# Transposing k and q by DMA instead of on TensorE in a sliding-window attention and gated feed-forward kernel

## The chip, the cores and the metric

The kernel runs on one core of one Trainium2 chip. The time is the device time of one execution in microseconds (us). The kernel before takes 276.5 us (median of its first three runs, 276.16 to 277.33). Smaller is better. On one core a single run has no second core to be compared with, so a run counts as undisturbed ("fast") unless it is over 1.5% above the fastest of its kernel. All ratios below use fast runs; a median quoted is that of all runs (e1, e8, e12 and e13 have one slow run each).

## The reference, cut to what matters

```python
B, H, S, D = 4, 8, 768, 64           # batch, heads, sequence, head width
scores = q @ k.T / sqrt(D)           # kept where key < 4 (the sink) or 0 <= query - key < 128 (the window)
a = softmax(scores)                  # a row at a time
x = (a @ v)                          # heads side by side: 3072 tokens x 512
out = (relu(x @ w_gate) * (x @ w_val)) @ w_out     # 512 -> 1536 -> 512
```

Inputs and outputs are float32. The kernel computes in bfloat16 with float32 accumulation.

## The kernel before

The attention is cut into units of one head pair each. Units 0 to 7 are the first batch in two halves, kinds "L" and "M". Units 8 to 19 are the twelve head pairs of the other three batches, kind "F", and only these change. For each unit the queue of the sync engine (SP) loads float32 k, q and v. GpSimd casts them to bf16. TensorE transposes k and q, so that the head width lies on the partitions, and ScalarE copies the result out of PSUM:

```python
def load_kq(self, eng):                       # partition p holds n consecutive tokens: pieces of n*64*4 B
    ...
        eng.dma_start(out=dst[0:pp, :, :],
                      in_=x[b, 2*p:2*p+2, r0:r0+pp*nn, :].rearrange("h (p n) d -> p h (n d)", n=nn))

def T(self, pool, shape, tag, qcopy=nc.scalar.copy):
    both = pool.tile(shape, BF16, name="tkq", tag=tag)
    for t in range(kn_): nc.tensor.transpose(ps[:, ...], self.kn_[0:kp, t, :, :]..., ident[0:kp, 0:kp])
    for t in range(qn_): nc.tensor.transpose(pq[:, ...], self.qn_[0:qp, t, :, :]..., ident[0:qp, 0:qp])
    nc.scalar.copy(kT[s]..., ps...)
    qcopy(qT[s]..., pq...)
    ...                                       # VectorE copies the keys that share a tile with the sink: kTs
```

The attention of a unit is a list of stages. Stages are placed between the chunks of the feed-forward (96 chunks; a chunk is four gate and four value matmuls) by a plan. `PLAN` holds pairs (chunk, number of stages issued by then):

```python
def t():
    if nxt is not None: nxt.T(*AT)            # transpose the next unit
    if x >= 5: held(x + 8 - 5)                # a memset on VectorE, then the load of unit x+3
    if at(x + 3) is not None: casts(at(x + 3), "kqv")
    if NP < x < NP + 4: load_wo(x - NP - 1)   # a third of the output weights, cast by the DMA, from GpSimd
...
return [s(0), v, s(1), t, s(2), lambda: norm(u, 0)]      # kind "F"; v ends the unit before
PLAN = ((0, 0), (2, 0), (10, 19), (23, 43), (47, 67), (71, 89), (72, 90))
```

`kT`, `qT` and `kTs` have two buffers each. Scores, outputs and transposes share two PSUM buffers ("at").

The softmax here doesn't subtract the row's maximum and nothing guards it: scores larger than these inputs give would overflow.

Of the kernel before, what the change touches and what calls it, by code (L numbers as in the profile page):

```python
# [43 lines left out]
def kernel(  # L44
# [12 lines left out]
    nc = tc.nc  # L57
    B, H, S, D = q.shape
# [23 lines left out]
    kT = [const.tile([128, 872], BF16, name=f"kT{i}") for i in range(2)]  # L82
    kTs = [const.tile([128, 3, 128], BF16, name=f"kTs{i}") for i in range(2)]
    qT = [const.tile([128, S], BF16, name=f"qT{i}") for i in range(2)]
# [11 lines left out]
    def bc(ap, n):  # L96

        return bass.AP(ap.tensor, ap.offset, [ap.ap[0], [0, n], *ap.ap[1:]])

    class Unit:  # L100
# [26 lines left out]
        def load_kq(self, eng):  # L127

            b, p = self.b, self.p
            for x, dst, r0, pp, nn in ((k, self.staging("k"), self.kr, self.kp, self.kn),  # L130
                                       (q, self.staging("q"), self.qr, self.qp, self.qn)):
                eng.dma_start(out=dst[0:pp, :, :],
                              in_=x[b, 2 * p:2 * p + 2, r0:r0 + pp * nn, :].rearrange("h (p n) d -> p h (n d)", n=nn))

# [29 lines left out]
        def sinkv(self, eng):  # L164

            t = self.sink
            src = vsink[:, self.p, :, :] if self.kind == "M" else self.vn[0:4, 0, :, 0:64]
            eng.tensor_copy(self.vn[0:4, t[0]:t[-1] + 1:2, :, 0:64], bc(src, len(t)))

        def T(self, pool, shape, tag, qcopy=nc.scalar.copy):  # L170

# [88 lines left out]
    def load_wo(c):  # L260
        nc.gpsimd.dma_start(out=wo[:, 4 * c:4 * c + 4, :],
                            in_=moe_w_out.rearrange("(ko ki) n -> ki ko n", ki=128)[:, 4 * c:4 * c + 4, :])
# [37 lines left out]
    def norm(u, part, pool=ps_at):  # L300

        c0, w = u.parts[part][0:2]
        nb = w // 32
        lo, hi = (max(c0, u.q0), min(c0 + w, u.q0 + u.n))
        o, sums = u.V(part, pool)
        r = rpool.tile([128, 2, 416], F32, name="R")
        rc = dpool.tile([128, 13], F32, name="rc")
        nc.vector.transpose(r[:, 0, 0:w], sums[:, 0:w])  # L308
        nc.vector.reciprocal(rc[:, 0:nb], r[:, 0, 0:w].rearrange("p (b j) -> p b j", j=32)[:, :, 0])  # L309
        a = rc[:, 0:nb]  # L310
        nc.vector.transpose(r[:, 1, 0:w], bass.AP(a.tensor, a.offset, [a.ap[0], [1, nb], [0, 32]]))  # L311
        ready[u.b, u.p] = hi
        nc.vector.tensor_tensor(xTs[u.b][:, u.p, lo:hi], o[:, lo - c0:hi - c0], r[:, 1, lo - c0:hi - c0], op=Alu.mult)  # L313
# [36 lines left out]
    with tc.manual_schedule():  # L350
# [3 lines left out]
        AT = (ps_at, [128, 2, 1024], "at")  # L354

        def at(x):
            return U[x] if 0 <= x < len(U) else None

        def casts(u, what):
            for w in what:  # L360
                u.cast(w, nc.gpsimd)
# [15 lines left out]
        def held(x):  # L377

            if x < len(U):
                nc.vector.memset(U[x].stg[0:1, 0:1], 0.0)  # L380
                load(x)
# [62 lines left out]
        def unit_stages(x):  # L444
            u, prev, nxt = U[x], at(x - 1), at(x + 1)

            def s(gi):
                def f():
                    if gi == 0 and u.kind == "F" and u.p == 0:
                        xTs[u.b] = xpool.tile([128, NP, S], BF16, name="xT")  # L450
                    u.S(gi)
                return f

            def v():
                if x > NP:
                    norm(prev, len(prev.parts) - 1)

            def t():
                if nxt is not None:
                    nxt.T(*AT)  # L460
                if x >= 5:
                    held(x + 8 - 5)
                if at(x + 3) is not None:
                    casts(at(x + 3), "kqv")
                if NP < x < NP + 4:
                    load_wo(x - NP - 1)
            if u.kind == "M":
                return [s(0), v, t, s(1)]
            return [s(0), v, s(1), t, s(2), lambda: norm(u, 0)]
# [9 lines left out]
        HALF = {0: ((0, 376), (376, 392))}  # L479
        ORDER = [(0, h, m) for h, m in [(h, m) for h in range(2) for m in range(FM)]]  # L480
        ORDER += [(b, h, m) for b in range(1, B) for h in range(2) for m in range(FM)]
        PLAN = ((0, 0), (2, 0), (10, 19), (23, 43), (47, 67), (71, 89), (72, 90))

        def want(ci):
            for (c0, w0), (c1, w1) in zip(PLAN, PLAN[1:]):
                if ci <= c1:
                    return w0 + (w1 - w0) * (ci - c0) // (c1 - c0)
            return total
# [56 lines left out]
```

## Time and profile before

| Engine | busy us of 273.9 | share |
|---|---|---|
| TensorE (PE) | 259.8 | 95% |
| VectorE (DVE) | 148.2 | 54% |
| ScalarE (ACT) | 129.6 | 47% |
| GpSimd (POOL) | 67.8 | 25% |

These are the busy times of one profiled execution. A TensorE at 95% only says where to look: matmuls overlap, so what an instruction really takes of TensorE is read from the start of one group to the start of the next. The DMA engines are the other thing to watch. They are nearly always busy until 68 us, and after 94 us they are mostly idle.

### The profile page before, as it was taken

The page shows a single profiled execution, that of the slowest core. Times are in us where ns is not written, and L with a number is a line of the kernel's source. Part 1 is how long each engine was busy: PE and PEld are TensorE (multiplying, and loading weights), DVE is VectorE, ACT ScalarE, POOL GpSimd, SP SyncE. Part 2 cuts the span into 40 slices and gives each one's busy share as a digit, 9 for nine tenths or more (in the row PEclk, how much of TensorE's full clock was granted, in tenths as well). Part 3 has the DMA queues.
Part 4 walks back from the last instruction along what each step waited for, and adds up shares of the span by engine and source line. Part 5 has one row for each costly group of instructions (what it writes and reads, how often), then busy time and mean ns, then how long its engine had stood idle before and what let it go on. Part 6 is the DMA issues. An engine that isn't in the chain of part 4 may idle for free.

```text
span 273.9 us, 5552 instructions
## 1 busy us (share of the span) xinstructions
PE 259.8 (95%) x2158; PEld 148.4 (54%) x2158; DVE 148.2 (54%) x329; ACT 129.6 (47%) x218; POOL 67.8 (25%) x123
## 2 busy tenths in 40 slices
PE   5997899899989999999999999999999999999994
PEld 4564555555545555555565555555655555555541
DVE  2486355778797755465666646565474722222210
ACT  3743656666646544536435363644535333323321
POOL 7973547653441330030402105000000000000000
PEclk9999999999999999999999999999999999999999
DMA  8999999998465170531707125101101110011122
GB/s 196 260 224 207 246 255 231 254 251 189 114 172 162 54 212 10 159 84 44 209 4 212 41 75 142 38 0 41 38 2 38 41 38 10 28 42 38 38 77 78
DMA packets 46858, 31.20 MB, mean 114 GB/s; under 512 B 28400, under 2 KB 43760, under 8 KB 46832
## 3 DMA queue, kind: packets, MB, share of 16 engines
q1 hardware_dynamic: 40224, 25.93, 34.2%
q0 software_dynamic: 5808, 4.72, 11.0%
q8 instruction: 17, 0.28, 0.4%
q10 hardware_dynamic: 800, 0.20, 0.3%
q14 instruction: 9, 0.07, 0.1%
HBM read 29.26 MB, written 6.29 MB: 130 GB/s over the span
## 4 chain that ended last, share of the span: by engine, by line
PE 84%; DVE 8%; ACT 3%; issue 1%; DMA 1%; POOL 1%; SPq 0%; DVEq 0%; ACTq 0%
PE gp L323 22%; PE op L342 22%; PE vp L329 21%; PE ops L248 7%; PE sps L226 5%; PE sps L221 2%; DVE R L311 2%; PE tkq L180 2%; DVE R L308 2%; PE tkq L183 2%; DVE xT L313 2%; ACT ee L230 2%; DMA stg<-in_q_dram 1%; DVE ee L232 1%; DVE rc L309 1%
## 5 line engine op out<-in xcount | busy, mean ns | idle before, releaser
L326 ACT ACTIVATE gs<-gp 128x384 f32<-128x384 f32 (+2 forms) x96 | 47.3, 493 | 73.2 <-PE gp L323 71.4
L323 PE MATMUL gp<-xT,wg 128*128 128x384 bf16 (+2 forms) x384 | 78.8, 327 | 1.4 <-DVE xT L313 1.4
L331 DVE TENSOR_TENSOR hT<-gs,vp 128x384 bf16<-128x384 f32 (+2 forms) x96 | 52.7, 549 | 49.3 <-PE vp L329 42.1
L329 PE MATMUL vp<-xT,wv 128*128 128x384 bf16 (+2 forms) x384 | 78.1, 326 | 0.0
L342 PE MATMUL op<-wo,hT 128*128 128x512 bf16 x288 | 75.9, 379 | 0.0
L230 ACT ACTIVATE ee<-sps 128x1006 bf16<-128x1006 f32 (+4 forms) x52 | 46.3, 905 | 26.5 <-PE sps L226 26.5
L329 PEld LDWEIGHTS <-wv 128*128 128x128 bf16 x384 | 37.6, 98 | 26.4 <-issue 1.6
L323 PEld LDWEIGHTS <-wg 128*128 128x128 bf16 x384 | 32.5, 98 | 25.2 <-issue 4.3
L342 PEld LDWEIGHTS <-hT 128*128 128x128 bf16 x288 | 28.2, 98 | 25.1
L232 DVE TENSOR_TENSOR ee<-ee,msk 128x1006 bf16<-128x1006 bf16 (+2 forms) x36 | 26.0, 723 | 26.0 <-ACT ee L230 25.8
L153 POOL CAST kn<-stg 128x768 bf16<-128x768 f32 (+2 forms) x20 | 15.4, 768 | 72.9 <-DMA stg<-in_k_dram 48.7
L346 ACT COPY ot<-op 128x512 f32<-128x512 f32 x24 | 14.1, 586 | 21.6 <-PE op L342 21.5
L308 DVE STREAM_TRANSPOSE R<-ops 128x384 f32<-128x384 f32 (+1 forms) x28 | 16.4, 584 | 14.3 <-PE ops L248 14.3
L186 ACT COPY kT<-tkq 128x768 bf16<-128x768 bf16 (+2 forms) x20 | 14.0, 700 | 18.1 <-PE tkq L183 17.9
L157 POOL CAST vn<-stg 128x768 bf16<-128x768 f32 (+2 forms) x20 | 14.4, 720 | 22.7 <-DMA stg<-in_v_dram 16.7
L311 DVE STREAM_TRANSPOSE R<-rc 128x384 f32<-128x384 f32 (+1 forms) x32 | 18.6, 582 | 1.1
L248 PEld LDWEIGHTS <-ones 128*64 128x64 bf16 x280 | 12.1, 109 | 12.3 <-issue 7.4
L313 DVE TENSOR_TENSOR xT<-ops,R 128x384 bf16<-128x384 f32 (+2 forms) x32 | 17.8, 557 | 1.4
L226 PEld LDWEIGHTS <-kT 64*128 64x128 bf16 x136 | 6.6, 93 | 19.2 <-issue 16.8
L248 PE MATMUL ops<-ee,ones 128*64 128x251 bf16 (+9 forms) x256 | 14.3, 238 | 2.2 <-DVE xT L313 1.3
L226 PE MATMUL sps<-qT,kT 64*128 64x251 bf16 (+3 forms) x136 | 15.5, 250 | 0.8 <-ACT qT L188 0.8
L153 POOL CAST qn<-stg 128x768 bf16<-128x768 f32 (+2 forms) x20 | 14.5, 724 | 5.2 <-DMA stg<-in_q_dram 4.8
(53 smaller groups left out, 169.8 us busy)
## 6 DMA issues: line engine op xcount, KB each, us to landing
out_dram<-ot SPq DMA_DIRECT2D x24, 256.0 KB
stg<-in_k_dram SPq DMA_DIRECT2D x12, 384.0 KB
stg<-in_q_dram SPq DMA_DIRECT2D x12, 384.0 KB
stg<-in_v_dram SPq DMA_DIRECT2D x24, 192.0 KB
wg<-in_moe_w_gate_dram POOLq DMA_DIRECT2D x4, 384.0 KB, 9.7
wv<-in_moe_w_val_dram POOLq DMA_DIRECT2D x4, 384.0 KB, 11.8
wo<-in_moe_w_out_dram POOLq DMA_DIRECT2D x3, 512.0 KB, 5.9
stg<-in_k_dram SPq DMA_DIRECT2D x4, 280.0 KB
```

Of the source, the lines that this page charges most:

```text
L153: cp(dst[0:pp, 0:nn, :, :], self.staging(what)[0:pp, :, :].rearrange("p h (n d) -> p n h d", d=64))
L226: nc.tensor.matmul(out=ps[:, h, c:c + w], lhsT=self.kw(j, r), rhs=qT[s][r, qa:qa + w], start=not biased, stop=True, skip_group_check=True)
L230: nc.scalar.activation(x, ps[:, :, 0:c], Act.Exp, bias=0.0, scale=scale)
L232: nc.vector.tensor_tensor(x, x, bc(msk[:, m0:m0 + c], 2), op=Alu.mult)
L248: nc.tensor.matmul(out=ps[1 - what][64 * h:64 * h + 64, qa - q0:qa - q0 + w], lhsT=self.vn[:, j, h, :] if what else ones[:], rhs=ee[s][:, ...
L311: nc.vector.transpose(r[:, 1, 0:w], bass.AP(a.tensor, a.offset, [a.ap[0], [1, nb], [0, 32]]))
L313: nc.vector.tensor_tensor(xTs[u.b][:, u.p, lo:hi], o[:, lo - c0:hi - c0], r[:, 1, lo - c0:hi - c0], op=Alu.mult)
L323: nc.tensor.matmul(out=gp[:, 0:n], lhsT=wg[:, ko, m * 128:(m + 1) * 128], rhs=x[:, ko, c0:c0 + n], start=ko == 0, stop=ko == KO - 1)
L326: nc.scalar.activation(gs[:, 0:n], gp[:, 0:n], Act.Relu, bias=0.0, scale=1.0)
L329: nc.tensor.matmul(out=vp[:, 0:n], lhsT=wv[:, ko, m * 128:(m + 1) * 128], rhs=x[:, ko, c0:c0 + n], start=ko == 0, stop=ko == KO - 1)
L331: nc.vector.tensor_tensor(hT[:, m, c0:c0 + n], gs[:, 0:n], vp[:, 0:n], op=Alu.mult)
L342: nc.tensor.matmul(out=op, lhsT=hTs[b][:, m, t * 128:(t + 1) * 128], rhs=wo[:, m, :], start=m == 0, stop=m == FM - 1)
```

## The change

Its intent is to take the 144 transposes off TensorE and the 24 copies off ScalarE. A DMA transposes each unit's k, and another its q, from SBUF to SBUF. So that the result has its columns in the order of tokens, partition p must hold tokens p, 128+p, 256+p and so on, and so the load of k and q now reads pieces of one token (64 floats, 256 B).

```diff
@@ load_kq
+                if self.kind == "F":
+                    eng.dma_start(out=dst.rearrange("p h (t d) -> p (h t) d", d=64),
+                                  in_=x[b, 2 * p:2 * p + 2].rearrange("h (t p) d -> p (h t) d", p=128))
+                    continue
@@ new methods of a unit
+        def X(self):
+            for x, dst in ((self.kn_, kT[self.s]), (self.qn_, qT[self.s])):
+                nc.sync.dma_start_transpose(out=dst[:, 0:S].rearrange("d (t r) -> d t r", r=128),
+                                            in_=x[:].rearrange("r t h d -> r (t h d)"))
+        def sinkk(self):
+            ...                      # the two copies into kTs, on VectorE, as before
@@ stage s(0) of unit u
+                    if gi == 0 and nxt is not None and nxt.kind == "F":
+                        nxt.X()
@@ stage t
-                    nxt.T(*AT)
+                    if nxt.kind == "F":
+                        nxt.sinkk()
+                    else:
+                        nxt.T(*AT)
-        PLAN = ((0, 0), (2, 0), (10, 19), (23, 43), (47, 67), (71, 89), (72, 90))
+        PLAN = ((0, 0), (2, 0), (11, 19), (23, 42), (47, 66), (71, 89), (72, 90))
```

More of the change, by code (lines that the diff above doesn't have):

```diff
@@ L168, in sinkv @@
             eng.tensor_copy(self.vn[0:4, t[0]:t[-1] + 1:2, :, 0:64], bc(src, len(t)))
+        def X(self):
[3 more added lines that the diff above has]
+        def sinkk(self):
+            s, nt = self.s, len(self.sink)
+            c = 124 * self.sink[0] + 4
+            a = kT[s][:, c:c + 124]
+            nc.vector.tensor_copy(kTs[s][:, 0:nt, 4:128],
+                                  bass.AP(a.tensor, a.offset, [a.ap[0], [248, nt], [1, 124]]))
+            nc.vector.tensor_copy(kTs[s][:, 0:nt, 0:4], bc(kT[s][:, 0:4], nt))
         def T(self, pool, shape, tag, qcopy=nc.scalar.copy):
```

## The prediction

> **What bounds the kernel now.** I read the page's first two parts, then the busy time of each engine in four stretches, then TensorE's timeline, and last the timelines of the DMA-issuing queue and of GpSimd. The page first: TensorE is busy 95% of the span, and no other engine is over 54%.
>
> ```profile
> span 273.9 us, 5552 instructions
> PE 259.8 (95%) x2158; PEld 148.4 (54%) x2158; DVE 148.2 (54%) x329; ACT 129.6 (47%) x218; POOL 67.8 (25%) x123
> ...
> PE   5997899899989999999999999999999999999994
> ...
> DMA  8999999998465170531707125101101110011122
> ```
>
> The average hides three regimes. The stretches show them (columns: window in us, length, busy us of each engine with its instruction count, clock, DMA share, GB/s):
>
> ```profile
> 45.00:94.00 49.00, 45.74 (x480) 27.70 (x480) 40.01 (x86) 29.43 (x43) 22.81 (x36) 1.00 0.76 187
> 94.00:193.00 99.00, 99.00 (x812) 55.30 (x810) 56.50 (x121) 47.91 (x79) 16.22 (x25) 1.00 0.30 88
> 193.00:274.00 81.00, 77.06 (x491) 41.61 (x488) 28.31 (x55) 27.64 (x51) 0.00 (x0) 1.00 0.11 40
> ```
>
> From 94 to 193 us TensorE never stops: 99.00 of 99. Whatever is taken off it there comes off the time one for one. From 45 to 94 us it lacks 3.26 us, VectorE is 82% busy (40.01 of 49), and the DMA engines are at 76%. After 193 us there is no transpose and no unit left to load, so nothing of the change reaches that stretch.
>
> **What one unit's transposes cost on TensorE.** The change removes them for the 12 whole-batch units (6 of k and 6 of q each; 144 in all). Durations in the table of groups (219 ns for one) overlap, so I read start to start:
>
> ```profile
> 109.44 1.03 PE L342 MATMUL op<-wo,hT 128*128 128x512 bf16 x4
> 110.30 0.50 PE L180 MATMUL tkq<-ident,kn 128*128 128x128 bf16 x6
> 110.64 0.50 PE L183 MATMUL tkq<-ident,qn 128*128 128x128 bf16 x6
> 110.97 0.81 PE L323 MATMUL gp<-xT,wg 128*128 128x384 bf16 x4
> ```
>
> From 110.30 to 110.97 is 0.67 us for 12, or 56 ns each, a quarter of the busy time shown. The weights group that follows starts without a gap. So the gain on TensorE is 12 x 0.67 = 8.0 us, of which seven units (those at 93.65 us and later, to 192 us) lie in the saturated stretch: 7 x 0.67 = 4.7 us. Five lie before it: 3.3 us.
>
> **What the Trainium skill says, and whether the trace agrees.** "VectorE: DVE Perf Modes", section "The three transpose paths", gives 390 ns for a 128x128 bf16 transpose on TensorE and 1309 ns by DMA. The first is for one in isolation; here a stream of them costs 56 ns each, so the measurement decides and the expected gain is much smaller than 144 x 390 ns. The second cannot be checked: no DMA here transposes. "DMA: Bandwidth & Descriptors", section "Latency and other measured facts", gives 261 GB/s for a DMA transpose with a non-contiguous middle dimension; a k or q of one unit is 128 x 768 x 2 B = 197 KB, so 0.75 us of data as an estimate from that page, and with its fixed cost of about 2 us (section "Anatomy of one DMA") about 3 us to landing. If 1309 ns were the price of every block, it would be 6 x 1.31 = 7.9 us. I take 1 to 1.5 us of DMA time each. Section "Queues, rings and completion order" says that a ring's descriptors are consumed in order. That matters: loads, transposes and stores are all issued from one queue, so a transpose waits for the data of the load issued ahead of it. No trace of before can show this for a transpose.
>
> **The change part by part.**
> Removed from TensorE: 8.0 us as above. Removed from ScalarE: 12 copies of kT at 0.798 us and 12 of qT at 0.805 us, 19.2 us; ScalarE is at 47%, so this is beside the path. VectorE's copies into the sink tiles stay, as many as before.
>
> PSUM: the transposes took a turn in the two-buffer pool that scores and outputs use. In the dense stretch they had to wait for it:
>
> ```profile
> 81.12 0.27 PE L226 MATMUL sps<-qT,kTs 64*128 64x248 bf16 x2
> 82.03 0.49 PE L180 MATMUL tkq<-ident,kn 128*128 128x128 bf16 x6 [0.65 <-DVE xT L313]
> ```
>
> Between 71 and 92 us I count five such gaps of about 0.7 us (a group of four score matmuls then takes 0.86 to 1.05 us until the next group, not 0.32), 3.5 us in all. Working out the old and the new plan chunk by chunk: the old one puts the stages of units 10 and 11 in pairs (second scores, transpose), (third scores, first norm), (first scores, second norm); the new one in pairs (second norm, second scores), (load stage, third scores), (first norm, first scores). With the transpose's turn gone and a feed-forward chunk now between the two norms, I expect most of the 3.5 us to go.
>
> Loads: k and q of these units now land in pieces of 256 B, not 1536 B. From the DMA packets between 100 and 190 us: 4 units' k and q in 2048 packets of 1536 B took 9.6 us x 16 engines, so 1.2 us per tensor; v in 256 B packets took 1.84 us for the same 393 KB. So +0.65 us per tensor, +1.3 us per unit.
>
> The path through the DMA queue, in the order of issue: the sink copy of unit y-1 on VectorE, a memset after it, load of y+1, transposes of y, sink copy of y. Now the load of a unit:
>
> ```profile
> 65.11 0.37 SPq L132 DMA_DIRECT2D stg<-in_k_dram  x1
> ...
> 69.04 0.93 POOL L153 CAST kn<-stg 128x768 bf16<-128x768 f32 x1 [4.20 <-DMA stg<-in_k_dram]
> 70.16 0.83 POOL L153 CAST qn<-stg 128x768 bf16<-128x768 f32 x1 [0.18 <-DMA stg<-in_q_dram]
> 71.35 0.83 POOL L157 CAST vn<-stg 128x768 bf16<-128x768 f32 x1 [0.37 <-DMA stg<-in_v_dram]
> ```
>
> Issued at 65.11, v usable at 71.35: 6.2 us. With the small pieces 7.5 us; k's transpose lands 1 to 1.5 us behind it, at 8.5 to 9 us, and q's at 9.5 to 10.5. The transposes of units 9 to 13 begin at 53.8, 62.5, 71.9, 82.0 and 93.7 us, so a unit now takes 8.7 to 11.7 us there. Without transposes and gaps TensorE would want one in some 8.3 us (three chunks of about 1.8 us plus 2.45 us of attention, and the switches). There the transposes come 0.5 to 2 us late, VectorE stops at the sink copy, and after the three buffers of gate and value are full TensorE stops too. Units 9 to 12 at about 1 us each: 4 us lost; unit 8, with weight loads on the same engines, perhaps 1 us more. After 94 us a unit takes 16 us, and the path hides entirely.
>
> Sum: 276.5 - 4.7 (late units) - 3.3 (early units) - 3.0 (most of the PSUM gaps) + 4.0 + 1.0 (late transposes) = 270.5. The lost time is my worst-known term, and the author moved the plan to suit; I lean 1 us lower: **269.5 us**.
>
> **The rivals.**
> 1. The transposes hide everywhere. For: TensorE has slack of three stages before the sink copy, and the plan starts attention one chunk later. Against: the loads queued ahead. Then 276.5 - 8.0 - 3.0 = 265.5.
> 2. The DMA queue becomes the bound of the dense stretch. For: 76% DMA share from 45 to 94 us, and 2 x (0.65 + 1 to 1.5) us more per unit. Against: GB/s there is only 187, under the 250 reached from 40 to 60 us. If each transpose takes 3 us, units 8 to 12 need about 12 us each against 8.3: the early gain turns into a loss, and the time is 274 to 277.
> 3. A transpose costs 7.9 us: two per unit plus a load is 23 us, over the 16 us of the saturated stretch too; 12 units at 7 us or more slower, over 330 us. Against: the page's own 261 GB/s, and that it would hardly have been tried with a fitted plan.
>
> **Range and chances.** Rival 1 sets the lower end, rival 2 the upper: 264.5 to 275. The 2% line is 271.0, near the middle of my uncertainty about the lost time. Faster by over 2%: 0.60; within 2%: 0.35; slower: 0.05, which is rival 3.
>
> **What would show each step.** Right: 144 fewer TensorE matmuls; between about 94 and 190 us TensorE still fully busy, and a unit 0.67 us shorter; no PSUM gaps like that at 82.03; small idle times of VectorE ended by the k transpose's DMA, in units 8 to 12 only. Wrong: waits of 2 us or more of VectorE for kT in each unit, TensorE idle after 94 us, or transposes with over 2 us of DMA time. If the early stretch has no such waits at all, rival 1 holds.

## The result, and the profile after

The changed kernel takes 285.21 us (median of 4 runs, 283.81 to 287.17) against 276.46. The ratio is 1.032 (95% interval 1.025 to 1.039), so it is slower by 3%. A ratio here is the mean time of one kernel's fast runs over that of the other's of the same rounds, and so not quite the ratio of the medians quoted. The outputs are correct.

The page of the changed kernel, with the same lines as the prediction shows of before, and the line of the granted clock:

```profile
span 282.7 us, 5228 instructions
...
PE 255.5 (90%) x1989; PEld 142.1 (50%) x2014; DVE 146.2 (52%) x329; ACT 112.1 (40%) x194; POOL 69.4 (25%) x123
...
PE   5996998094978979999999999999999999999994
...
PEclk9999999668699999999999999999999999999999
DMA  8999999995999999929296884914101000011012
```

The weight loads (PEld) fell from 2158 to 2014: the 144 transposes are gone. (TensorE's own count is 25 lower still: the output matmuls are 263 in place of 288. These are records missing from the trace.) ScalarE lost 17.5 us. But TensorE now has slices of 0, 4 and 7 tenths between 48 and 85 us, and its clock drops to 6 tenths in slices where it was 9. The last line says that the DMA engines, which after 68 us stood at 0 to 7 tenths before, are now near their limit up to some 120 us.

The stretches (us of the window, its length, busy us of each engine with its count, clock, DMA share, GB/s), first the two of the prediction, then the two longest stops and what follows each:

```profile
45.00:94.00 49.00, 34.08 (x287) 18.57 (x288) 26.25 (x60) 16.00 (x24) 16.85 (x26) 0.83 0.94 173
94.00:193.00 99.00, 96.69 (x769) 52.81 (x780) 61.02 (x135) 41.08 (x69) 23.96 (x35) 1.00 0.80 137
...
48.10:55.99 7.89, 0.09 (x7) 0.03 (x1) 1.07 (x5) 0.86 (x1) 3.08 (x5) 0.74 1.08 171
56.00:61.20 5.20, 5.20 (x36) 2.63 (x36) 3.07 (x7) 1.50 (x2) 1.59 (x3) 0.50 0.92 149
66.40:70.40 4.00, 0.06 (x4) 0.03 (x1) 1.44 (x5) 0.00 (x0) 3.03 (x5) 0.82 0.60 121
70.40:75.90 5.50, 5.49 (x34) 2.75 (x34) 3.43 (x7) 1.51 (x2) 0.00 (x0) 0.51 0.90 146
```

TensorE stands still for 7.9 us and again for 4.0 us, and after each stop it works for over 5 us at half the clock (0.50 and 0.51). Its timeline names what it waits for. Compare the four score matmuls at 60.69, still at the low clock, with those of later units: 0.53 us until the next group (at 61.22) against 0.32.

```profile
48.01 0.18 PE L245 MATMUL sps<-qT,kT 64*128 64x20 bf16 x2
55.99 0.40 PE L245 MATMUL sps<-qT,kT 64*128 64x255 bf16 x2 [7.80 <-DMA qT<-qn]
...
58.07 1.44 PE L342 MATMUL gp<-xT,wg 128*128 128x376 bf16 x4
59.29 1.46 PE L348 MATMUL vp<-xT,wv 128*128 128x376 bf16 x4
60.69 0.39 PE L245 MATMUL sps<-qT,kT 64*128 64x251 bf16 x2
60.87 0.41 PE L245 MATMUL sps<-qT,kTs 64*128 64x248 bf16 x2
...
70.41 0.40 PE L245 MATMUL sps<-qT,kT 64*128 64x255 bf16 x2 [3.95 <-DMA qT<-qn]
```

Both wait for the DMA transpose of q, for units 8 and 9. Four gate matmuls take 1.44 us here and 0.80 us at full clock.

**Where the time went.** I compared when each chunk starts in the two traces. Up to the start of the 25th chunk (91.47 us before, 104.74 after) the changed kernel loses 13.3 us. From there to the end (182.4 us before, 177.9 after) it gains 4.5 us. The difference is the 8.8 us between the spans.

- Lost: stops of 7.80 (unit 8), 3.95 (unit 9), 1.56, 1.40 and 1.65 us (units 10 to 12; each is the excess of a group of attention-output matmuls' start-to-start time over 0.71 us), 16.4 us in all. Then 11.6 us of work at half the clock (the low clock lasts until 62.2 and until 75.8 us), which at full clock takes half of that, so 5.8 us.
- Gained: five units' transposes, 3.3 us, and the PSUM gaps of about 0.7 us, which are gone (from 76 us on such a group of score matmuls takes 0.32 us each time). The prediction counted five; the trace of before has four, ending at 71.87, 78.30, 82.03 and 88.46 us, 2.7 us in all.
- Also gone are five waits of 0.21 to 0.61 us between 32 and 50 us, 1.9 us in all, among the units of the first batch, which the new plan spaces otherwise. And the new plan has issued one stage fewer by that chunk (0.3 us).
- The sum is 14.0 us; measured are 13.3. I do not assign the 0.7 us between.

### The profile page after: what moved, and what is told of

It reads as the page before. It is cut to its first block, busy times and chain, and to the rows that moved or that the text cites. A ratio compares the mean times of both kernels' runs of the same rounds, so it can differ in the third digit from the quotient of the medians.

```text
span 282.7 us, 5228 instructions
## 1 busy us (share of the span) xinstructions
PE 255.5 (90%) x1989; PEld 142.1 (50%) x2014; DVE 146.2 (52%) x329; ACT 112.1 (40%) x194; POOL 69.4 (25%) x123
## 2 busy tenths in 40 slices
DMA packets 96778, 35.91 MB, mean 127 GB/s; under 512 B 84464, under 2 KB 93680, under 8 KB 96752
## 4 chain that ended last, share of the span: by engine, by line
PE 73%; DMA 15%; SPq 4%; DVE 3%; POOL 2%; issue 1%; ACT 0%; POOLq 0%; DVEq 0%; ACTq 0%
PE gp L342 20%; PE op L361 20%; PE vp L348 19%; DMA stg<-in_k_dram 7%; DMA kT<-kn 5%; PE ops L267 5%; PE sps L245 4%; SPq L146 3%; PE sps L240 2%; DMA qT<-qn 1%; DMA stg<-in_q_dram 1%; POOL kn L157 1%; PE tkq L199 1%; PE warm L389 1%; PE tkq L202 1%
## 5 line engine op out<-in xcount | busy, mean ns | idle before, releaser
L342 PE MATMUL gp<-xT,wg 128*128 128x384 bf16 (+2 forms) x384 | 80.6, 333 | 1.4 <-DVE xT L332 1.4
L348 PE MATMUL vp<-xT,wv 128*128 128x384 bf16 (+2 forms) x384 | 79.5, 331 | 0.0
L361 PE MATMUL op<-wo,hT 128*128 128x512 bf16 x263 | 71.9, 381 | 1.1
L251 DVE TENSOR_TENSOR ee<-ee,msk 128x1006 bf16<-128x1006 bf16 (+2 forms) x36 | 24.2, 673 | 27.7 <-ACT ee L249 27.7
L245 PE MATMUL sps<-qT,kT 64*128 64x251 bf16 (+3 forms) x136 | 16.0, 255 | 17.4 <-DMA qT<-qn 16.2
L327 DVE STREAM_TRANSPOSE R<-ops 128x384 f32<-128x384 f32 (+1 forms) x28 | 16.4, 586 | 13.9 <-PE ops L267 13.9
L267 PE MATMUL ops<-ee,vn 128*64 128x144 bf16 (+9 forms) x280 | 16.1, 242 | 0.1
L267 PE MATMUL ops<-ee,ones 128*64 128x251 bf16 (+9 forms) x256 | 15.0, 246 | 0.0
```

The costliest lines, as they stand in the source:

```text
L245: nc.tensor.matmul(out=ps[:, h, c:c + w], lhsT=self.kw(j, r), rhs=qT[s][r, qa:qa + w], start=not biased, stop=True, skip_group_check=True)
L251: nc.vector.tensor_tensor(x, x, bc(msk[:, m0:m0 + c], 2), op=Alu.mult)
L267: nc.tensor.matmul(out=ps[1 - what][64 * h:64 * h + 64, qa - q0:qa - q0 + w], lhsT=self.vn[:, j, h, :] if what else ones[:], rhs=ee[s][:, ...
L342: nc.tensor.matmul(out=gp[:, 0:n], lhsT=wg[:, ko, m * 128:(m + 1) * 128], rhs=x[:, ko, c0:c0 + n], start=ko == 0, stop=ko == KO - 1)
L348: nc.tensor.matmul(out=vp[:, 0:n], lhsT=wv[:, ko, m * 128:(m + 1) * 128], rhs=x[:, ko, c0:c0 + n], start=ko == 0, stop=ko == KO - 1)
L361: nc.tensor.matmul(out=op, lhsT=hTs[b][:, m, t * 128:(t + 1) * 128], rhs=wo[:, m, :], start=m == 0, stop=m == FM - 1)
```

## The experiments

Every kernel here was timed in three rounds beside the kernel before, and each gave a correct result. Theory A, formed after reading the trace: the transposes are late because of where they stand, behind the loads in one queue and beside the output-weight loads, not because of the work itself. The rivals are named with the runs. The edits are shown cut.

**e1: only the loads in small pieces.** The kernel before, plus:

```diff
+                if self.kind == "F":          # load_kq: pieces of 256 B, as in the change
+                    eng.dma_start(out=..., in_=x[...].rearrange("h (t p) d -> p (h t) d", p=128)); continue
-            nc.scalar.copy(kT[s]... rearranged)         # T(): the copies become plain, for kind "F"
+            nc.scalar.copy(kT[s][:, 0:S], ps[:, 0:S])
```

> The kernel before with one part of the change alone: k and q of the whole-batch units are loaded in pieces of 256 B (TensorE still transposes). Theory A (the transposes sit in one queue behind the loads, and pieces of 256 B get a small share of the DMA engines beside the weight loads' packets of 1024 B; the loads alone have a lead of some two units and hide): within 1 us of before, 275.5 to 277.5. Rival B (the small pieces themselves are what costs the time): most of the 9 us, 281 to 286.

Measured: 278.64 us, ratio 1.005 (1.002 to 1.009). The half percent is a little over what theory A allowed, but the small pieces alone are not the loss.

**e8: only the transposes, with nobody waiting.** The kernel before, plus the two DMA transposes of each unit at the same places in the order, into tiles that nothing reads.

> The kernel before, and in addition the change's DMA transposes of every whole-batch unit, at the same places in the order, into tiles that nothing reads; loads in pieces of 1536 B and TensorE's transposes stay. Nobody waits for the transposes, so only their load on the DMA engines and on the queue counts. Theory A (a matter of waiting in the wrong place): 276 to 279. Rival C (load on the engines): 281 or more.

Measured: 283.55 us (280.67 to 286.24), ratio 1.021 (1.015 to 1.027). So theory A as I had put it is wrong: the transposes cost time, on the engines and in the queue, even if nobody waits for what they write. In the profiled run (the fastest of the four; span 278.9, which is 5.0 us over before) every chunk starts within 0.2 us of before up to one place, and there all of it is lost, the low clock after the stop included:

```profile
67.29 0.83 PE L337 MATMUL vp<-xT,wv 128*128 128x392 bf16 x4
72.29 0.39 PE L350 MATMUL op<-wo,hT 128*128 128x512 bf16 x1 [4.17 <-DMA wo<-in_moe_w_out_dram]
```

TensorE waits for the last third of the output weights. GpSimd issued that load at 63.00 us, not at 59.31 as before, because it stood for 4.05 us in front of the cast of a v that came late. The transposes delayed the loads, the loads delayed GpSimd, and GpSimd issues the weights.

e1 and e8 also bound what is left. By the ratios they cost 1.4 and 5.8 us. If these simply added to the 8.0 + 2.7 us that TensorE saves, the changed kernel would take some 273 us, as an estimate. It takes 285, so some 12 us are the waiting for the transposed tiles and what follows from it.

**e7: the old plan.** The changed kernel with the PLAN line of before.

> The changed kernel with the old plan. Theory A: the old plan asks for the transposed tiles a chunk earlier in the dense stretch, so the stops grow: 285 to 289. Rival D (the later plan is what costs the time, as fewer chunks stand between the stages): 278 or less.

Measured: 284.50 us, ratio 1.030 (1.025 to 1.035), not to be told from the changed kernel's 1.032. The plan is neither the cause nor the cure. The first stop did grow, as I expected, from 7.80 to 9.40 us, but the second fell from 3.95 to 1.83, and the time did not grow.

**e2: transposes from another queue.**

```diff
-                nc.sync.dma_start_transpose(
+                nc.scalar.dma_start_transpose(
```

> The changed kernel with the transposes issued from ScalarE's queue instead of the one that issues the loads, so that they need not wait for the data of the load issued before them. Theory A (the wait is the place behind the load): the three long stops of TensorE between 47 and 76 us shrink to under 2 us each, and the time is 268 to 276. Rival C (the DMA engines are at their limit there, 0.94 busy from 45 to 94 us): the transposes come as late as before, 282 to 287. ScalarE issues each for 1.2 us and waits for the cast, which may cost 1 to 3 us.

Measured: 279.20 us, ratio 1.011 (1.005 to 1.016), between the two expectations. The place behind the loads costs part of the loss: unit 8's k transpose is issued at 43.95 us, not at 48.98, and the stop at unit 8 is 1.98 us, not 7.80 (a wait of 1.21 us for ScalarE comes before it). The trace puts no wait of TensorE down to the transposed tiles any more, but TensorE waits twice for the output weights instead (1.87 and 6.82 us). Relieved in one place, the same collision shows in another.

**e4: lead time and a looser loop.** Three buffers, loads a unit earlier, and the transposes of unit y issued together with the load of unit y+2, which need no longer wait for the sink copy of unit y. (The order in the queue stays what it was: load of y+1, transposes of y, load of y+2; the load of unit 9, the transposes of unit 8 and the load of unit 10 start at 43.63, 48.98 and 55.70 us in the changed kernel and at 43.02, 48.41 and 52.17 here.)

```diff
-    kT / kTs / qT: range(2), index i % 2          +    range(3), index i % 3
 stage s(0): -   nxt.X()
 stage t:
-                if x >= 5: held(x + 8 - 5)
+                if at(x + 2) is not None and at(x + 2).kind == "F": at(x + 2).X()
+                if x >= 4: held(x + 4)
```

> The changed kernel with three buffers for the transposed k, q and sink tiles, each load one unit earlier, and the transposes of a unit issued a unit earlier and ahead of the next load. Theory A (order in the queue and lead time): no wait of VectorE or TensorE for the transposed tiles over 1 us after 50 us, and the gain that was predicted, 264 to 271. Rival C (DMA engines at their limit): the same bytes have to move in the same time, waits of several us stay, 278 or more.

Measured: 277.86 us, ratio 1.004 (1.001 to 1.006). This is 7.4 us better than the changed kernel, still 7 us short of theory A, and just under the 278 of rival C. After the first stop (9.2 us, unit 8) only stops of 1.0 to 1.3 us are left: from the start of the 13th chunk to that of the 25th it takes 36.1 us; the changed kernel takes 43.5, the kernel before 36.6.

**e6 and e9: the output weights early.** The three loads are issued right behind the other weights. In e6 this is done to the changed kernel, in e9 to e4's kernel.

```diff
 stage t: -   if NP < x < NP + 4: load_wo(x - NP - 1)
 before the stages: +   for c in range(3): load_wo(c)
```

> The changed kernel with the three loads of the output weights issued right behind the other weights, before 30 us, in place of beside units 8 to 10. Theory A (packets of 256 B lose the engines to packets of 1024 B while a weight load runs: in the changed kernel the load queue moves some 70 packets in 0.5 us then, against 400 to 500 without): the stops at 48, 66 and 74 us shrink to under 3 us each, and the time is 273 to 280. Rival C (all bytes of the dense stretch have to pass, whatever their order): 283 to 287, as the weights then delay the units' loads before.

> The kernel with three buffers, early loads and transposes ahead of the load, with the output weights early as well. It waited 10 us for unit 8 alone, in which the transposes were in flight beside an output-weight load. Theory A: that wait goes to under 3 us, and the time is 266 to 271. Rival C: 276 to 279.

Measured: e6 281.28 us, ratio 1.016 (1.014 to 1.019); e9 278.17 us, ratio 1.005 (1.002 to 1.008). Theory A misses both: e6 lies between its two expectations, e9 in the range of rival C. In e6 the stop of unit 9 is gone, as theory A said, but that of unit 8 has grown from 7.80 to 13.26 us (12.62 in e9):

```profile
48.07 0.18 PE L245 MATMUL sps<-qT,kT 64*128 64x20 bf16 x2
61.51 0.40 PE L245 MATMUL sps<-qT,kT 64*128 64x255 bf16 x2 [13.26 <-DVE hT L350]
```

(hT stands on VectorE behind the sink copy, which waits for the transposed k.) The weight loads now run beside the load of unit 8. The queue shows it (start, duration of the issue): the load keeps the issuing engine for 9.24 us, while its queue moves some 150 packets in a us (42 to 48 us).

```profile
38.27 4.05 SPq L133 DMA_DIRECT2D stg<-in_q_dram  x1
42.41 9.24 SPq L146 DMA_DIRECT2D stg<-in_v_dram  x2
```

The collision moves with the weights. I therefore counted packets, in slices of one us, in the packet records of the traces. While both queues have work, each moves about the same number of packets, whatever their size (in the first row one of them was not busy all the time):

| kernel, us | unit loads' queue: packets, GB/s | weights' queue: packets, GB/s |
|---|---|---|
| before, 57 to 58 (mostly 1536 B) | 84, 98 | 118, 110 |
| changed, 51 to 52 (256 B) | 141, 35 | 157, 161 |
| e12 (below), 22 to 23 (256 B) | 189, 47 | 191, 143 |
| e12, 44 to 45 (1536 B) | 113, 166 | 108, 104 |
| changed, 46 to 47 (256 B, no weights) | 1085, 274 | 0, 0 |

The Trainium skill says this in "DMA: Bandwidth & Descriptors", section "Queues, rings and completion order": an engine goes round the queues that have work, packet by packet. The counts agree, for what the trace records as packets (a packet of the page may hold several of these). With packets of 256 B against 1024 B, the loads and the transposes behind them get about a fifth of the bytes until the weights have passed, 35 GB/s here in place of some 220 to 270.

**e10: weights in small packets too.** The changed kernel with each output-weight load cut into four along its columns.

```diff
-        nc.gpsimd.dma_start(out=wo[:, 4*c:4*c+4, :], in_=...[:, 4*c:4*c+4, :])
+        for i in range(4):
+            nc.gpsimd.dma_start(out=wo[:, 4*c:4*c+4, i*128:(i+1)*128], in_=...[:, 4*c:4*c+4, i*128:(i+1)*128])
```

> The changed kernel with each of the three output-weight loads cut into four whose packets are 256 B, not 1024 B, so that a turn of either queue on an engine moves the same bytes. Theory A (engines take turns packet by packet): while such a load runs, the unit loads' queue moves over 80 GB/s, not the 35 GB/s of the changed kernel at 51 us, the transposes of unit 8 land earlier, and the first stop (8.4 us) shrinks by 2 us or more; the time 276 to 283, less certain, since the weights come later and GpSimd issues nine DMAs more (7 us in all). Rival C (bytes alone): the same 35 GB/s share of time lost, first stop over 8 us, 285 or more.

Measured: 281.95 us, ratio 1.021 (1.015 to 1.026), in the range of theory A. From 52 to 53 us the two queues move 365 and 366 packets, 92 and 89 GB/s: the share is as theory A says. But the first stop shrank by 0.4 us only (7.38 us), not by 2 us. In other slices the unit loads' queue had little to offer (139 packets against 539 from 51 to 52 us). So the taking of turns is real and costs part of the time; it is not what makes most of the first stop. Much of the rest of that stop is the queue itself: in e2, with the weights beside them but from another queue, the transposes were issued 5 us earlier and the stop was 1.98 us. In the chain of work of the changed kernel (start, duration, what), the transposes of unit 8 are issued only at 48.98, when the load of unit 9 has been put out, and k's lands 6.19 us later:

```profile
48.98 6.19 DMA kT<-kn
...
66.18 2.75 DMA kT<-kn
...
78.23 3.46 DMA kT<-kn
...
82.16 4.96 DMA stg<-in_k_dram
...
87.80 3.10 DMA kT<-kn
```

The next three take 2.75 to 3.5 us to land, with no weights beside them.

**e3: only the late units.** The kernel before with its plan; DMA transposes and small loads for units 13 to 19 only.

```diff
-                if self.kind == "F":         (in load_kq, stage s(0) and stage t)
+                if self.dmat:                # self.dmat = i >= 13
```

> The kernel before and its plan, with DMA transposes (and their 256 B loads) for units 13 to 19 only, TensorE's transposes for units 8 to 12. All theories put the loss before the 24th chunk; the seven late units should keep 7 x 0.67 = 4.7 us, so 271 to 273. If it is 275 or more, the removal of TensorE's transposes is worth less than the trace says.

Measured: 270.91 us, ratio 0.980 (0.977 to 0.984), so about 2% faster, not surely over 2%. By the means of the fast runs it gains 5.5 us. This holds what TensorE's start-to-start times promised for the late units (4.7 us) and about 0.8 us more, which I do not assign.

**e13 and e11: from unit 11 on.** The first three whole-batch units run beside the output-weight loads. e13 is the changed kernel with `self.dmat = i >= 11` and nothing else (units 8 to 10 also get their loads in 1536 B back); e11 is e4's kernel with the same condition.

> The changed kernel, its order in the queue and its two buffers as they are, but DMA transposes from unit 11 on only (units 8 to 10 as before). With the changed kernel (285), three buffers for all units (278) and three buffers from unit 11 (269) it completes a table of two by two. Theory A': both matter. The three units that run beside the output-weight loads cost most, and the place behind the load costs some 1 to 2 us for each of units 11 to 13: 271 to 275, with waits of 1 to 3 us of TensorE at units 11 to 13. If the order is all that matters: 277 or more. If the units are all that matter: 268 to 270.

> A version meant to beat both: three buffers, loads one unit early, transposes ahead of the next load, and DMA transposes from unit 11 on, when the output weights have landed; units 8 to 10 keep TensorE's transposes and loads of 1536 B. Theory A: no stop over 1.5 us for the transposed tiles; against before 9 x 0.67 = 6.0 us less and most PSUM gaps of units 10 and 11 gone: 266 to 270. Rival C: waits of some us at units 11 and 12, 272 to 276.

| | all twelve units | from unit 11 on |
|---|---|---|
| the change's two buffers and lead | 285.21 (the change) | 269.71 (e13) |
| three buffers, loads and transposes earlier | 277.86 (e4) | 268.97 (e11) |

The ratios to before are 1.032, 1.004, 0.975 (0.972 to 0.978) and 0.974 (0.968 to 0.979). I had expected that both matter; the table says that with the first three units left to TensorE the lead hardly matters. It is worth 7.4 us in the left column, and in the right column the two cannot be told apart. (The place behind the load is not tested by this table, as it is the same in both rows; e2 tests it.) In e11, no engine waits for a transposed tile: the list of who waits for these DMAs, under "who waited", is empty (columns: engine, operation, count, lowest, median and highest ns of one, first and last start).

```profile
L179 SPq DMA_TRANSPOSE kT<-kn x9: 1226/1262/2198, 68.9 to 169.1; - x9
L179 SPq DMA_TRANSPOSE qT<-qn x9: 1222/1238/1246, 71.2 to 170.4; - x9
its engine sat idle before it (us, times) until:
who waited for it (us, times):
```

and its page shows a TensorE that is kept busy at the full clock:

```profile
PE   5997899889999999999999999999999999999994
...
PEclk9999999999999999999999999999999999999999
```

e11 and e13 beat both kernels.

**e12: from unit 10 on, weights early.** e11's kernel with `i >= 10` and the early weights of e6.

> The same with DMA transposes from unit 10 on and the output weights loaded early, behind the other weights. The early weights starved the load of unit 8 when it came in pieces of 256 B (a stop of 13 us); with pieces of 1536 B it should keep up. Theory A: 264 to 269, the best of all. If the weights still starve the load of unit 8 whatever its pieces, a stop of over 5 us at 48 us, and 270 to 276.

Measured: 271.26 us (270.35 to 277.92), ratio 0.981 (0.974 to 0.989), under neither expectation cleanly. Pieces of 1536 B keep up better beside the weights (the fourth row of the table of packets), and at 46 us TensorE waits 0.46 and 1.81 us, not 13. Still it is not better than e11.

## Why the prediction was wrong, point by point

**Right: what a transpose is worth on TensorE.** The late stretch gained 4.5 us where 7 x 0.67 = 4.7 was predicted, and e3 kept more than that. After 102 us TensorE stayed full. (Of the 2.31 us that it lacks between 94 and 193 us, 1.59 are the stop of unit 12, which ends at 101.73; the rest goes with the missing records.)

**Right in kind: the PSUM gaps.** All are gone in the changed kernel. But they were four and 2.7 us, not five and 3.5, and two of the four (78.30 and 88.46) ended in attention outputs, not in transposes. The 3.0 us written was near by luck.

**Right: the DMA time of a transpose.** I took 1 to 1.5 us. The 24 transposes of e8 raise the busy time of the loads' queue, as the pages give it for all 16 engines, from 34.2% of 273.9 us to 45.2% of 278.9 us, 1.35 us each. Packets rose from 46858 to 96778 in the changed kernel, that is 24 tensors by 1280 more pieces and 24 transposes by 800. Rival 3 (7.9 us for each) is dead. The small pieces cost more than the 0.65 us that I wrote for a tensor: e1's 42.3% of 275.4 us makes it 0.95.

**Right only for the later units: the path.** I had k's transposed tile 8.5 to 9 us after the issue of the load ahead of it. For unit 11 it was 8.7 us (82.16 to 90.89), but for units 8 to 10 it was 11.5, 13.2 and 11.8 us (from the loads at 43.63, 55.70 and 69.92 to the tiles at 55.17, 68.93 and 81.69). "Units 9 to 12 at about 1 us each" was near for units 10 to 12 (1.4 to 1.65 us), for unit 10 by luck.

**Wrong: the term "+ 4.0 + 1.0 (late transposes)".** These 5.0 us were the step that failed: they measured 16.4 us of stops and 5.8 us lost at half clock. The stops also came another way than written. TensorE waited itself, at its first scores of a unit, for the transposed q (16.2 us in five waits), not for gate and value buffers that VectorE had failed to empty. Three things were missing in the term.

1. *The first units, beside the output-weight loads.* "Unit 8, with weight loads on the same engines, perhaps 1 us more" was the worst part: unit 8 lost 7.80 us and unit 9 3.95. I had counted bytes and the mean DMA share (76%), and I had not asked what a queue of 256 B packets gets beside one of 1024 B, nor how long the load ahead holds the queue. e13 shows that the loss lies in these units: leave units 8 to 10 to TensorE, change nothing else, and 285.21 becomes 269.71. It does not single out the weights beside them: e6 and e9 moved the weights, and they then met the load of unit 8 instead. How the stop of unit 8 divides between the packets' turns and the queue ahead is not settled: e10 took the unequal turns away and recovered 0.4 us of it; e2 took the queue ahead away and recovered 5.8.
2. *Lateness feeds itself.* The next load is issued after a memset that stands behind the sink copy on VectorE, and that copy waits for the transpose:

```profile
55.20 0.33 DVE L185 COPY kTs<-kT 128x372 bf16<-128x372 bf16 x1 [6.82 <-DMA kT<-kn]
...
55.59 0.06 DVE L399 MEMSET stg<- 1x1 f32 x1
...
55.70 0.38 SPq L133 DMA_DIRECT2D stg<-in_k_dram  x1
```

I had written down this path and taken its length as harmless. Once late, each unit starts the next load late. e4, which loosens the loop by a unit, is 7.4 us faster.
3. *The clock.* I did not consider that a stop lowers TensorE's clock. "TensorE: Matmul & The Clock Gate" of the Trainium skill, section "Why this matters for your kernels", warns of idle gaps over some 3 us and of a return to half clock; the stops of 7.80 and 3.95 us were followed by 0.50 and 0.51, and those of 1.4 to 1.65 us in this kernel were not followed by any drop. Other runs do not bear out a limit of 3 us: stops of 2.61 us (e13), 1.81 us (e12) and 1.75 us (e6, at 98 us) were each followed by some 3.4 us at 0.50 or 0.51, while 2.62 us (e7, at 78 us) and 1.87 us (e2, at 63 us) were not. What decides is not shown. In e13, the gate matmuls before and after the stop:

```profile
65.34 0.84 PE L343 MATMUL gp<-xT,wg 128*128 128x392 bf16 x4
...
69.45 1.01 PE L362 MATMUL op<-wo,hT 128*128 128x512 bf16 x2 [2.61 <-DMA wo<-in_moe_w_out_dram]
...
72.19 1.01 PE L343 MATMUL gp<-xT,wg 128*128 128x392 bf16 x4
```

Of the rivals, the second ("the DMA queue becomes the bound of the dense stretch") named what happened, with 274 to 277 where 285 was measured, though not for its reason (a transpose takes 1.35 us of DMA time, not 3). I gave it too little because the GB/s of before were below what the engines reach; the loss came from who gets the engines and the queue and when, and e8 shows that the added work alone, with nobody waiting for its result, costs 2%.

## What to carry to other kernels

Work that moves from a full engine to the DMA pays where the DMA is idle and the consumer is far off; in this kernel the same change gains 2.5% when it is confined to units 11 to 19 and loses 3.2% when it includes units 8 to 10. Before you shrink the pieces of a load, look at what else is in flight then and with which packet size, and at what stands behind it in the queue. Count what a stop of TensorE costs afterwards: in the changed kernel the two long stops cost about 3.1 and 2.7 us more at half clock, the three short ones nothing; in other runs a stop of 1.75 to 2.61 us could cost half of some 3.4 us in the same way.

## What the Trainium skill lacked or had wrong

- "DMA: Bandwidth & Descriptors" states that engines go round the queues packet by packet, but not what follows for the bytes: 141 packets of 256 B moved 35 GB/s beside 157 packets of the weights' queue at 161 GB/s (changed kernel, 51 to 52 us); at 1536 B, 84 packets moved 98 GB/s.
- The same page has no measured issue time for one DMA transpose from SBUF to SBUF of this size: 1.22 to 1.27 us for 128 x 768 bf16 when undisturbed, with 800 packets; k's landed 2.75 to 3.5 us after its issue in the three cases of the changed kernel's chain without a weight load beside them. The 1309 ns of "VectorE: DVE Perf Modes" for 128 x 128 are no price for each block: six blocks took 1.35 us of DMA time (e8).
- None of the pages that I read says that a load of many small pieces can hold the issuing engine: two v loads took 9.24 us to issue in e6, beside the weights, and 1.0 to 1.7 us in the kernel before.
- "TensorE: Matmul & The Clock Gate", section "Why this matters for your kernels", puts the gap that costs the clock at some 3 us; here 1.75, 1.81 and 2.61 us did it (e6, e12, e13), while 2.62 us in e7 did not.
- "TensorE: Matmul & The Clock Gate", section on PE-mode transpose, gives 275 ns for a transpose in a kernel's context; here one lasts 219 ns, and in a stream of twelve they follow each other every 56 ns.
